# A planner's numbers for transfers are raised: longer issues, later landings of spreads and raw weights

## The chip, the cores and the metric

The kernel runs on one core of a Trainium2 chip. The metric is the time of one execution on the device, in microseconds (us). The core has five engines that work side by side, each through its own list of instructions, strictly in order: PE (matrix products), DVE (vector), ACT (activations), POOL (vector too, slower), and SP, which here only issues transfers (DMAs). An instruction whose input isn't ready holds up everything behind it on its engine.

## What is computed

```python
q_rot, k_rot = rotate(q), rotate(k)                    # 4 batches x 8 heads, 576 rows, 64 wide
attn = softmax(q_rot @ k_rot.T / sqrt(64)); a = attn @ v
x = a as [2304, 512]                                   # tokens x (heads * 64)
r = maximum(x @ w_in, 0.0);  g = s * (r * r) + b       # d_ff = 2048
x = g @ w_out
out = (silu(x @ w_gate) * (x @ w_val)) @ w_out2        # d_ff = 1536
```

## The kernel before

All products are made in pieces that keep nearly full precision: a number is split in a high part (hi) and a remainder (lo), and a product is two or three matmuls.

Attention works on 16 pairs of heads, pair 0 to pair 15. `prep` (a pair's preparation) loads q and k, rotates them (POOL from pair 1 on), transposes them on PE (pst, L515) and splits them: qkhi on ACT (L524), qklo on DVE (L526). Both lie in buffers of which there is one each. From there ten transfers on SP, the pair's *spread* (L548), copy the parts to where PE reads them: a, t and kz, two sets, used by even and odd pairs. The next pair's qkhi may be written only when the spread has landed; the token `hi` stands for that buffer. A spread also waits until the scores of two pairs before have been computed, since they read the same set.

`pair` then runs nine score blocks per pair: score matmuls into ps_s (L620), the row maximum nm on DVE (L623), the exponential e on ACT (L627). The probabilities are transposed on PE (ps_t, L681), split into ph on ACT (L689) and pl on DVE (L696), and multiplied with v (ps_av, L711), which ACT takes out as xr (L724) and SP stores to x_d (L732). The three PSUM banks of ps_t serve the transposes of q and k too.

The weights come as raw 64-bit numbers (`fetch`, L289 and L291, three raw buffers); ACT and DVE decode them (L304 to L315). Ten of the first MLP's are fetched during attention. The first MLP runs in five blocks of tokens; its input for the first block, xl and xh of 1 MB each, is loaded during attention (L762). The second MLP runs in three blocks.

The order is not written by hand. The kernel first describes every operation with its engine, a duration, what it needs, which buffers it takes and a priority (`op`, `dma`). `Schedule.run` then plays through them by these numbers: whenever an engine is free by the plan, it emits the ready operation of the best priority. The plan thus fixes the order of each engine's list, and nothing else; on the chip each instruction goes as soon as what it waits for is there. For a transfer the plan has SP busy for a fixed time, adds 0.65 us and the size over 360 KB per us (one transfer after the other), and 1.3 us until it has landed. A large pace makes a transfer count as larger.

Of the kernel before, what the change touches and what calls it, by code (L numbers as in the profile page):

```python
# [17 lines left out]


class Op:  # L20
    __slots__ = ("eng", "dur", "lag", "fn", "need", "users", "prio", "acq", "rel", "port", "ready", "done", "size", "next")


class Token:
# [6 lines left out]
class Schedule:  # L31
# [5 lines left out]
    def __init__(self):  # L37
        self.free, self.ops = {}, []

    def dma(self, size, fn, prio, deps=(), acq=(), rel=(), after=(), pace=1.0, eng="sp"):  # L40

        o = self.op(eng, 0.55, fn, prio, deps, acq, rel)
        o.size = size * pace
        for d in after:
            d.next.append(o)
            o.need += 1
        return o
# [15 lines left out]
    def run(self):  # L63
        ready = {}
        seq = 0
        wait = []
        for o in self.ops:
            if o.need == 0:
                heapq.heappush(wait, (0.0, seq, o))
                seq += 1  # L70
        busy = {}
        port_until = dma_free = 0.0
        work = {}
        times = [0.0]
        emitted = 0
        gone = []
        while times:
            now = heapq.heappop(times)
            while times and times[0] <= now + 1e-9:
                heapq.heappop(times)  # L80
            while gone and gone[0][0] <= now + 1e-9:
                _, _, o = heapq.heappop(gone)
                for t in o.rel:
                    t.left -= 1
                    if t.left == 0:
                        self.free[t.pool] += 1
            while wait and wait[0][0] <= now + 1e-9:
                _, s, o = heapq.heappop(wait)
                heapq.heappush(ready.setdefault(o.eng, []), (o.prio, s, o))
            for eng in sorted(ready, key=str):  # L90
                while busy.get(eng, 0.0) <= now + 1e-9 and ready[eng]:
                    skipped, got = [], None
                    while ready[eng]:
                        item = heapq.heappop(ready[eng])
                        o = item[2]
                        ok, picks = not (o.port and busy.get("pool", 0.0) > now + 1e-9 or eng == "pool" and port_until > now + 1e-9), []
                        for t in o.acq if ok else ():
                            p = next((p for p in t.pools if self.free.get(p, 0) - sum(x == p for _, x in picks) > 0), None)
                            if p is None:
                                ok = False  # L100
                                break
                            picks.append((t, p))
                        if ok:
                            got = o
                            break
                        skipped.append(item)
                        if len(skipped) > 60:
                            break
                    for item in skipped:
                        heapq.heappush(ready[eng], item)  # L110
                    if got is None:
                        break
                    o = got
                    for t, p in picks:
                        t.pool = p
                        self.free[p] -= 1
                    o.fn()
                    emitted += 1
                    dur = o.dur
                    if eng == "pe":  # L120
                        tick = int(now / 3.4133)
                        if work.get(tick - 1, 0.0) < 1.275:
                            dur *= 2
                        at = now
                        while at < now + dur:
                            tick = int(at / 3.4133 + 1e-9)
                            to = min(now + dur, (tick + 1) * 3.4133)
                            work[tick] = work.get(tick, 0.0) + (to - at) * o.dur / dur
                            at = to + 1e-9
                    end = now + dur  # L130
                    busy[eng] = end
                    if o.port:
                        port_until = end
                    o.done = end + o.lag
                    if o.size is not None:
                        dma_free = max(dma_free, end + 0.65) + o.size / 360e3
                        o.done = dma_free + 1.3
                    heapq.heappush(times, end)
                    seq += 1
                    heapq.heappush(times, o.done + RL)  # L140
                    heapq.heappush(gone, (o.done + RL, seq, o))
                    hop = self.HOP[eng] + self.HX if o.size is None else 0.0
                    for u, t in [(u, o.done + ((0.0 if u.eng == "pe" else 0.06) if u.eng == o.eng else hop)) for u in o.users] + [(u, end) for u in o.next]:
                        u.need -= 1
                        u.ready = max(u.ready, t)
                        if u.need == 0:
                            seq += 1
                            heapq.heappush(wait, (u.ready, seq, u))
                            heapq.heappush(times, u.ready)
        assert emitted == len(self.ops), (emitted, len(self.ops))  # L150
# [27 lines left out]
def tile_attention_moe_moe(  # L178
# [43 lines left out]
    sch = Schedule()  # L222
# [11 lines left out]
    late = {}  # L234
# [40 lines left out]
    def fetch(key, prio, dep=None, after=(), acq=()):  # L275

        kind, f = key
        src = {"in": w_in, "out": w_out, "gate": w_gate, "val": w_val, "out2": w_out2}[kind]
        wide = src.dtype != F32
        n = 2 if wide else 1  # L280
        if wide:
            src = src.bitcast(U32)
        st = {}
        raw_tok = Token("raw")

        def load():
            st["raw"] = raw = raw_p.tile([128, n * 512], U32 if wide else F32, tag="raw", name="raw")
            if kind in ("out", "out2"):
                nc.sync.dma_start(out=raw, in_=src[f * 128:(f + 1) * 128, :])  # L289
            else:  # L290
                nc.sync.dma_start(  # L291
                    out=raw.rearrange("p (k m) -> p k m", k=KD),
                    in_=src[:, f * 128 * n:(f + 1) * 128 * n].rearrange("(k p) m -> p k m", p=128),
                )

        o = W_ld[key] = sch.dma(n * 262144, load, prio, (dep,), (raw_tok, *acq), after=after, pace=1.5)
        if wide:
            dec_tok = Token("dec")

            def d0():  # L300
                two = st["raw"].rearrange("p (m two) -> p m two", two=2)
                st["low"], st["high"] = two[:, :, 0], two[:, :, 1]
                st["t"] = dec_p.tile([128, 512], U32, tag="dec", name="dec")
                nc.scalar.activation(out=st["t"].bitcast(F32), in_=st["high"].bitcast(F32), func=AF.Copy, scale=2.0 ** -112)  # L304

            def d1():
                nc.vector.tensor_scalar(out=st["t"], in0=st["t"], scalar1=3, scalar2=None, op0=ALU.logical_shift_left)

            def d2():
                nc.vector.scalar_tensor_tensor(  # L310
                    out=st["t"], in0=st["high"], scalar=0x80000000, in1=st["t"], op0=ALU.bitwise_and, op1=ALU.bitwise_or
                )

            def d3():
                nc.vector.scalar_tensor_tensor(  # L315
                    out=st["t"], in0=st["low"], scalar=29, in1=st["t"], op0=ALU.logical_shift_right, op1=ALU.bitwise_or
                )
                st["val"] = st["t"].bitcast(F32)

            o = op("act", t_act(512, False), d0, prio, (o,), (dec_tok,))  # L320
            o = op("dve", t_dve2(512), d1, prio, (o,), port=True)
            o = op("dve", t_dve(512), d2, prio, (o,), port=True)
            o = op("dve", t_dve(512), d3, prio, (o,), (), (raw_tok,), port=True)
            end = (dec_tok,)
        else:
            st["val"] = None
            end = (raw_tok,)
        return st, o, end
# [95 lines left out]
    def prep(p):  # L424
# [120 lines left out]
        if p > 1:  # L545
            def sp(o, i, first=False):
                return sch.dma(
                    256 * o.shape[1], lambda: nc.sync.dma_start(out=o.bitcast(F32), in_=i().bitcast(F32)), pr + 6, (*trs, *zeros[z]),  # L548
                    (tok,) if first else (), (hi_tok,), pace=1.3
                )  # L550
            ops = []
            for s0, s1, d0 in a_pieces(0, 2 * S):
# [819 lines left out]
```

## Time and profile before

| | us |
|---|---|
| median of 3 runs | 1133.8 (1132.83 to 1136.26) |
| the profiled execution | 1131.5 |
| its span | 1129.7 |
| PE busy | 1100.3 (97%) |
| DVE busy | 798.7 (71%) |
| ACT busy | 591.6 (52%) |
| POOL busy | 190.6 (17%) |

Attention takes about the first 300 us. POOL and the 16 DMA engines are busiest there: the DMA engines' busy share is 0.80 from 30 to 210 us. A wait is told as "engine, line, what it waited for". The clock of PE is given as a share of 2.4 GHz; its two levels are 1.2 and 2.4 GHz, 0.5 and 1.0 in the rows.

### The profile page before, as it was taken

The numbers are of one execution on the slowest core, as the hardware profiler recorded it, in microseconds if no ns is written. First come the engines' busy times: TensorE is split into PE (matmuls) and PEld (weight loads), VectorE is DVE, ScalarE is ACT, GpSimd is POOL, SyncE is SP. The second block draws the span as 40 slices with busy tenths as digits, with TensorE's granted clock in tenths as the row PEclk, the third lists the DMA queues.
The fourth block names the chain that finished last, engine by engine and source line by source line (L and its number), as shares of the span: only waits on it lengthen the run. The fifth ranks groups of instructions, "written<-read, shape, count | busy, mean of one in ns | idle before, by whom it ended". The sixth has DMA issues, their size and how long they took to land. (4 is left out here: it accounts for less than half of the span.)

```text
span 1129.7 us, 17997 instructions
## 1 busy us (share of the span) xinstructions
PE 1100.3 (97%) x6314; PEld 1006.1 (89%) x6314; DVE 798.7 (71%) x1394; ACT 591.6 (52%) x1199; POOL 190.6 (17%) x156
## 2 busy tenths in 40 slices
PE   7999899999999999999999999999999999999998
PEld 6989898989888788888899999999979999899986
DVE  6989888999969867867768764555565555665560
ACT  5989788889878845544554543322242222422230
POOL 6776675743200000000000000000000000000000
PEclk9999999999999999999999999999999999999999
DMA  5588888777376477576576766766656552666501
GB/s 125 135 197 182 219 210 200 187 168 186 88 236 190 127 231 233 177 238 222 196 241 217 250 225 209 247 201 206 210 158 221 197 195 96 196 229 194 183 11 46
DMA packets 185721, 211.16 MB, mean 187 GB/s; under 512 B 71824, under 2 KB 121120, under 8 KB 185632
## 3 DMA queue, kind: packets, MB, share of 16 engines
q1 hardware_dynamic: 184192, 209.33, 61.9%
q8 instruction: 50, 0.82, 0.3%
q10 hardware_dynamic: 1440, 0.69, 0.2%
q14 instruction: 39, 0.32, 0.1%
HBM read 142.07 MB, written 47.26 MB: 168 GB/s over the span
## 5 line engine op out<-in xcount | busy, mean ns | idle before, releaser
L1242 DVE TENSOR_TENSOR tmp<-hb,tmp 128x384 f32<-128x384 f32 x252 | 140.0, 557 | 114.0 <-PE hb L812 112.7
L810 PE MATMUL hb<-xh,w 128*128 128x384 f32 (+1 forms) x560 | 199.0, 355 | 2.0 <-DVE pl L696 2.0
L812 PE MATMUL hb<-xh,w 128*128 128x384 f32 (+1 forms) x560 | 199.0, 355 | 0.0
L811 PE MATMUL hb<-xl,w 128*128 128x384 f32 (+1 forms) x560 | 198.8, 355 | 0.0
L811 PE MATMUL acc<-gl,w 128*128 128x512 f32 (+1 forms) x320 | 117.9, 368 | 0.1
L810 PE MATMUL acc<-gh,w 128*128 128x512 f32 (+1 forms) x320 | 117.9, 368 | 0.0
L812 PE MATMUL acc<-gh,w 128*128 128x512 f32 (+1 forms) x320 | 117.6, 368 | 0.0
L810 PEld LDWEIGHTS hb<-xh,w 128*128 128x128 f32 x560 | 105.1, 188 | 12.7 <-DVE pl L696 1.5
L623 DVE TENSOR_REDUCE nm<-ps_s 128x1 f32<-128x576 f32 x144 | 108.2, 752 | 9.8 <-PE ps_s L620 8.7
L811 PEld LDWEIGHTS hb<-xl,w 128*128 128x128 f32 x560 | 105.1, 188 | 10.4
L627 ACT ACTIVATE e<-ps_s,nm 128x576 f32<-128x576 f32 x144 | 107.0, 743 | 10.8 <-DVE nm L623 10.0
L812 PEld LDWEIGHTS hb<-xh,w 128*128 128x128 f32 x560 | 105.1, 188 | 8.3 <-DVE w L349 0.2
L689 ACT ACTIVATE ph<-ps_t 128x512 fp32r<-128x512 f32 x192 | 106.7, 571 | 8.4 <-PE ps_t L681 6.3
L620 PE MATMUL ps_s<-t,a 128*128 128x288 f32 x320 | 101.2, 332 | 7.8 <-ACT e L627 7.8
L696 DVE TENSOR_TENSOR pl<-ps_t,ph 128x512 fp32r<-128x512 f32 x144 | 95.9, 683 | 5.9 <-ACT ph L689 5.3
L711 PE MATMUL ps_av<-ph,vh 128*128 128x384 f32 (+1 forms) x320 | 98.1, 328 | 0.0
L1257 ACT ACTIVATE tmp<-tmp 128x384 f32<-128x384 f32 x72 | 37.8, 525 | 111.5 <-DVE tmp L1242 109.2
L681 PE MATMUL ps_t<-ident,e 128*128 128x128 f32 x576 | 86.8, 276 | 6.9 <-DVE qklo L526 4.1
L620 PE MATMUL ps_s<-kz,a 128*128 128x288 f32 x320 | 90.7, 299 | 0.1
L811 PE MATMUL hb<-w 128*128 128x384 f32 x264 | 88.9, 337 | 0.0
L812 PE MATMUL hb<-w 128*128 128x384 f32 x264 | 88.8, 337 | 0.0
L810 PE MATMUL hb<-w 128*128 128x384 f32 x264 | 88.5, 335 | 0.0
(118 smaller groups left out, 2298.9 us busy)
## 6 DMA issues: line engine op xcount, KB each, us to landing
w<-wd SPq DMA_DIRECT2D x120, 512.0 KB, 4.4
wd<-w SPq DMA_DIRECT2D x48, 512.0 KB, 3.4
raw<-in_moe_w_out_dram SPq DMA_DIRECT2D x28, 512.0 KB, 5.1
x_d<-xr SPq DMA_DIRECT2D x64, 144.0 KB, 2.8
w<-wd SPq DMA_DIRECT2D x36, 256.0 KB, 4.0
raw<-in_moe_w_in_dram SPq DMA_DIRECT2D x16, 512.0 KB, 4.2
raw<-in_moe_w_gate_dram SPq DMA_DIRECT2D x12, 512.0 KB, 6.1
raw<-in_moe_w_val_dram SPq DMA_DIRECT2D x12, 512.0 KB, 6.3
```

The costliest lines, as they stand in the source:

```text
L620: nc.tensor.matmul(ps[:, hf * 512:hf * 512 + HS], a[:, q0:q0 + 128], m[:, k0:k0 + HS], start=y == 0, stop=y == len(todo) - 1)
L623: nc.vector.tensor_reduce(out=st["nm"][:, u:u + 1], in_=st["s", u], axis=AX.XY, op=ALU.max, negate=True)
L627: nc.scalar.activation(out=st["e", u].rearrange("p (f n) -> p f n", f=2), in_=st["s", u], func=AF.Exp, bias=st["nm"][:, u:u + 1], accum_ou ...
L681: nc.tensor.transpose(ps[:, z * 128:z * 128 + 128], st["e", u][:, kc * 128:kc * 128 + 128], ident)
L689: nc.scalar.activation(out=st["ph", y][0:rows, 512 * i:512 * i + n], in_=st["pt", y, i][0:rows, 0:n], func=AF.Copy)
L696: nc.vector.tensor_tensor(out=dst, in0=st["pt", y, i][0:rows, 0:n], in1=st["ph", y][0:rows, c].bitcast(F32), op=ALU.subtract)
L711: nc.tensor.matmul(ps, vv, st["ph", y][:, c], start=kc == 0, stop=kc == 4)
L810: nc.tensor.matmul(o, lh, rh, start=first, stop=False)
L811: nc.tensor.matmul(o, lh, rl, start=False, stop=False)
L812: nc.tensor.matmul(o, ll, rh, start=False, stop=last)
L1242: nc.vector.tensor_tensor(out=st[dst, f], in0=ps[z], in1=st[a, f], op=ALU.add)
L1257: nc.scalar.activation(out=st[key, f], in_=st[key, f], func=AF.Silu)
```

## The change

Three numbers of the plan change. Every transfer keeps SP busy for 0.64 us instead of 0.55. A transfer can have a `late`, which is added to its landing: 2.0 us for the ten transfers of each spread and for each raw weight, 0 for the rest. No operation is added or taken away, and no wait that data or buffers don't ask for.

```diff
-    __slots__ = ("eng", "dur", "lag", "fn", "need", "users", "prio", "acq", "rel", "port", "ready", "done", "size", "next")
+    __slots__ = ("eng", "dur", "lag", "fn", "need", "users", "prio", "acq", "rel", "port", "ready", "done", "late", "size", "next")
...
-    def dma(self, size, fn, prio, deps=(), acq=(), rel=(), after=(), pace=1.0, eng="sp"):
-
-        o = self.op(eng, 0.55, fn, prio, deps, acq, rel)
-        o.size = size * pace
+    def dma(self, size, fn, prio, deps=(), acq=(), rel=(), after=(), pace=1.0, eng="sp", late=0.0):
+
+        o = self.op(eng, 0.64, fn, prio, deps, acq, rel)
+        o.size, o.late = size * pace, late
...
                         dma_free = max(dma_free, end + 0.65) + o.size / 360e3
-                        o.done = dma_free + 1.3
+                        o.done = dma_free + 1.3 + o.late
...
-        o = W_ld[key] = sch.dma(n * 262144, load, prio, (dep,), (raw_tok, *acq), after=after, pace=1.5)
+        o = W_ld[key] = sch.dma(n * 262144, load, prio, (dep,), (raw_tok, *acq), after=after, pace=1.5, late=2.0)
...
-                    (tok,) if first else (), (hi_tok,), pace=1.3
+                    (tok,) if first else (), (hi_tok,), pace=1.3, late=2.0
```

The order of nearly the whole of attention changes, in the MLPs little. Three places follow. The numbers behind the names are buffers' numbers.

ACT, around the qkhi of pair 4. In the old order qkhi_1014 belongs to pair 4, and e_1131 is the first exponential of pair 3 (nm_1101 is pair 3's):

```order
L524 ACTIVATE qkhi_1014<-pst_1021,qs_203 128x2x192
L627 ACTIVATE e_1036,l_373<-ps_s_1008,nm_820 128x576
L724 ACTIVATE xr_864<-ps_av_967 128x384
L524 ACTIVATE qkhi_1014<-pst_1040,qs_203 128x2x192
L689 ACTIVATE ph_992<-ps_t_1048 128x512
L627 ACTIVATE e_1073,l_373<-ps_s_1027,nm_820 128x576
L689 ACTIVATE ph_992<-ps_t_1062 64x384
L689 ACTIVATE ph_1090<-ps_t_1080 128x512
L627 ACTIVATE e_1099,l_373<-ps_s_1055,nm_820 128x576
L689 ACTIVATE ph_1090<-ps_t_1093 128x512
L689 ACTIVATE ph_1090<-ps_t_1110 128x512
L627 ACTIVATE e_1131,l_373<-ps_s_1102,nm_1101 128x576
```

In the new order qkhi_1094 is pair 4's and nm_1076 is pair 3's:

```order
L689 ACTIVATE ph_1061<-ps_t_1034 128x512
L627 ACTIVATE e_1069,l_371<-ps_s_1046,nm_823 128x576
L689 ACTIVATE ph_1061<-ps_t_1063 128x512
L524 ACTIVATE qkhi_1094<-pst_1084,qs_203 128x2x192
L524 ACTIVATE qkhi_1094<-pst_1089,qs_203 128x2x192
L627 ACTIVATE e_1108,l_371<-ps_s_1077,nm_1076 128x576
L724 ACTIVATE xr_1117<-ps_av_1053 128x384
L524 ACTIVATE qkhi_1094<-pst_1110,qs_203 128x2x192
```

The three qkhi of pair 4 stood before the last exponentials of pair 2; now they stand around the first of pair 3.

PE, the transposes of q and k of pair 4 (pst) and the scores around them; a0 and t0 hold pair 2 here, a1 and t1 pair 3. Before:

```order
L681 MATMUL ps_t_994<-ident_201,e_855 128x128
L681 MATMUL ps_t_994<-ident_201,e_890 128x128
L515 MATMUL pst_1000<-ident_201,x_623 128x2x64 x3
L620 MATMUL ps_s_1008<-t0_206,a0_204 128x288
L620 MATMUL ps_s_1008<-kz0_208,a0_204 128x288
L620 MATMUL ps_s_1008<-t0_206,a0_204 128x288
L620 MATMUL ps_s_1008<-kz0_208,a0_204 128x288
```

Now, with the first score block of pair 3 at its head:

```order
L620 MATMUL ps_s_1077<-t1_207,a1_205 128x288
L620 MATMUL ps_s_1077<-kz1_209,a1_205 128x288
L620 MATMUL ps_s_1077<-t1_207,a1_205 128x288
L620 MATMUL ps_s_1077<-kz1_209,a1_205 128x288
L515 MATMUL pst_1084<-ident_201,x_615 128x2x64 x3
L515 MATMUL pst_1089<-ident_201,x_615 128x2x64 x3
```

The transposes of pair 4 moved from between the scores of pair 2 to behind the first scores of pair 3.

SP, around the spread of pair 6 (a0, t0, kz0) and the load of the first MLP block's input (xl, xh). Before, its last transfers and what follows:

```order
L548 DMA t0_206<-qklo_1496 64x576
L548 DMA kz0_208<-qkhi_1495 64x576
L732 DMA x_d00_126<-xr_1393 64x576
L732 DMA x_d10_130<-xr_1393 64x576
L762 DMA xl_1759<-x_d00_126 128x4x512
L762 DMA xh_1758<-x_d10_130 128x4x512
L732 DMA x_d01_127<-xr_1662 64x576
L732 DMA x_d11_131<-xr_1662 64x576
L392 DMA x_1792<-in_q_dram 128x9x64
L392 DMA x_1792<-in_k_dram 128x9x64
```

Now, what stands ahead of the same spread and its first transfers:

```order
L732 DMA x_d00_126<-xr_1381 64x576
L732 DMA x_d10_130<-xr_1381 64x576
L448 DMA vr_1545<-in_v_dram 64x2x64
L392 DMA x_1623<-in_q_dram 128x9x64
L392 DMA x_1623<-in_k_dram 128x9x64
L762 DMA xl_1647<-x_d00_126 128x4x512
L762 DMA xh_1646<-x_d10_130 128x4x512
L548 DMA a0_204<-qkhi_1587 64x576
L548 DMA a0_204<-qklo_1588 64x576
```

The two large loads moved from behind the spread of pair 6 to ahead of it.

## Rows read from the trace of the kernel before

**Rows 1.** Busy time by stage: start:end, length, each engine, clock, DMA share, GB/s.
```profile
30.00:210.00 180.00, 169.94 (x1291) 162.04 (x1290) 154.64 (x246) 154.03 (x364) 126.18 (x95) 0.98 0.80 191
210.00:300.00 90.00, 87.44 (x665) 82.15 (x664) 88.41 (x145) 82.29 (x196) 38.31 (x34) 1.00 0.68 164
316.00:808.00 492.00, 491.95 (x2442) 440.72 (x2442) 346.38 (x629) 239.33 (x415) 0.00 (x0) 1.00 0.66 216
```

**Rows 2.** Waits of PE, 30 to 210 us: total, times, longest, in us.
```profile
PE ps_t L681 <- DVE qklo L526: 4.1, 3, 2.9
PE ps_s L620 <- ACT e L627: 3.1, 4, 1.9
PE pst L515 <- DVE qklo L526: 2.6, 1, 2.6
```

**Rows 3.** Waits of ACT, 30 to 210 us.
```profile
ACT qkhi L524 <- DMA kz<-qkhi: 3.9, 2, 3.1
...
ACT qkhi L524 <- DMA t<-qklo: 3.3, 1, 3.3
ACT dec L304 <- DMA raw<-in_moe_w_in_dram: 2.1, 1, 2.1
```

**Rows 4.** Timeline of PE: start, length, instruction, idle before it and its releaser.
```profile
129.54 0.60 PE L681 MATMUL ps_t<-ident,e 128*128 128x128 f32 x4
129.90 0.38 PE L620 MATMUL ps_s<-t,a 128*128 128x288 f32 x1
...
137.40 1.12 PE L681 MATMUL ps_t<-ident,e 128*128 128x128 f32 x4 [2.92 <-DVE qklo L526]
...
157.29 0.40 PE L620 MATMUL ps_s<-t,a 128*128 128x288 f32 x1 [1.86 <-ACT e L627]
```

**Rows 5.** Busy time and clock after the two stalls, columns as in rows 1.
```profile
136.00:144.00 8.00, 6.61 (x40) 6.33 (x40) 6.01 (x10) 7.21 (x17) 2.68 (x5) 0.79 0.84 197
156.00:164.00 8.00, 6.71 (x38) 6.44 (x39) 6.04 (x10) 6.48 (x17) 4.41 (x5) 0.79 0.66 140
```

**Rows 6.** Timeline of SP's queue around the spread of pair 6.
```profile
92.24 0.59 SPq L548 DMA_DIRECT2D kz<-qkhi  x1
...
99.87 0.78 SPq L392 DMA_DIRECT2D x<-in_k_dram  x1
...
103.08 0.60 SPq L548 DMA_DIRECT2D a<-qkhi  x1
...
108.86 0.60 SPq L548 DMA_DIRECT2D kz<-qkhi  x1
...
113.44 1.99 SPq L732 DMA_DIRECT2D x_d<-xr  x2
...
116.18 1.97 SPq L392 DMA_DIRECT2D x<-in_k_dram  x1
118.21 3.44 SPq L446 DMA_DIRECT2D vr<-in_v_dram  x1
...
123.02 0.62 SPq L444 DMA_DIRECT2D vr<-in_v_dram  x1
...
125.68 1.18 SPq L732 DMA_DIRECT2D x_d<-xr  x2
```

**Rows 7.** Line 548, the spreads: time from issue to landing.
```profile
DMA to landing us min/median/max: 2.4/3.0/5.3
```

**Rows 8.** ACT's instructions of attention: count, duration, and qkhi's first and last start.
```profile
L627 ACT ACTIVATE e<-ps_s,nm 128x576 f32<-128x576 f32 x144 | 107.0, 743 | 10.8 <-DVE nm L623 10.0
L689 ACT ACTIVATE ph<-ps_t 128x512 fp32r<-128x512 f32 x192 | 106.7, 571 | 8.4 <-PE ps_t L681 6.3
...
L724 ACT ACTIVATE xr<-ps_av 128x384 f32<-128x384 f32 x48 | 23.8, 497 | 0.5 <-PE ps_av L711 0.5
...
L524 ACT ACTIVATE qkhi<-pst,qs x42: 567/582/607, 36.3 to 262.6; 128x384 fp32r<-128x384 f32 x42
```

## The prediction

> **What bounds the kernel now.** I read the busy time by stage first, then PE's waits, then the waits of the engine that PE waited for, then SP's queue.
>
> The stages [rows 1]: from 316 to 808 us PE is busy for 491.95 of 492.00 us at the full clock. There no other order can save anything. Attention is different. From 30 to 210 us PE is busy for 169.94 of 180.00 us, so 10.06 us are idle, and the granted clock is 0.98. From 210 to 300 us it idles for 2.56 of 90.00 us. DVE is busy 154.64 of the 180 us, and 88.41 of the 90: behind PE it is the next limit.
>
> Who holds PE up between 30 and 210 us [rows 2]: 4.1 + 2.6 = 6.7 us end with qklo on DVE, and 3.1 us with the exponentials on ACT. These are chains. PE's transposes wait for a bank of PSUM that qklo has to empty, qklo waits for qkhi on ACT, and qkhi waits for a DMA: the previous pair's spread has not landed, and qkhi must overwrite the buffer that the spread reads. ACT's own list says so [rows 3]: 3.9 us for kz<-qkhi, 3.3 us for t<-qklo, and 2.1 us in which the decode waited for a raw weight. The largest of these stalls on PE are 2.92 us before 137.40 and 1.86 us before 157.29 [rows 4]. PE is slow after both: in the 8 us from 136 and the 8 us from 156 the mean granted clock is 0.79, partly the lower of its two levels [rows 5].
>
> SP is what makes the spreads late. From the first to the last of one spread's ten issues there are nine steps in 108.86 - 103.08 = 5.78 us, 0.64 us each [rows 6], where the plan of before reckons 0.55: 0.9 us too little for ten. A spread transfer lands a median of 3.0 us from its issue, 5.3 us at worst [rows 7].
>
> **The change part by part.** It adds no instruction; the planner only writes the same ones down in another order.
>
> *Spreads.* The planner now reckons 10 x 0.09 = 0.9 us more issue and 2.0 us more landing, so everything that needs a spread moves back by about 2.9 us. On ACT, between the last qkhi of pair 3 and the first of pair 4, the old order holds 1 qkhi, 8 ph, 6 e and 2 xr: 0.58 + 8 x 0.57 + 6 x 0.74 + 2 x 0.50 = 10.6 us [rows 8]. The new one holds 1, 11, 8 and 2: 13.8 us. That is 3.2 us more cover, and the wait there was the 3.1 us one [rows 3]. Pairs 3 to 5 had 10.6 to 11.7 us in this tally and have 13.8 now. On PE the new order puts the q and k transposes of pair p behind the first scores of pair p - 1, which need the spread of p - 1 complete. So qkhi can hardly wait for a landing any more. I count the whole 6.7 us as gone, and with the stall the slow clock after it: 8 x 0.21 = 1.7 us [rows 5]. Bounds: 0 (the wait moves to the scores) to 8.4 us; I take 8.4, since the added cover equals the measured wait.
>
> *Raw weights.* In the old order the first decode is ACT's next instruction behind the qkhi of pair 9. In the new one it stands nine instructions behind the qkhi of pair 8: 3 e, 5 ph, 1 xr, 5.6 us [rows 8], against a wait of 2.1 us [rows 3]. The PE stall of 1.86 us goes, and its clock, 1.7 us: 3.6 us, between 0 and 3.6. In the MLPs the same 2.0 us changes nothing that PE waits for [rows 1].
>
> *What comes late next.* First, the first MLP block's x: two transfers, xl and xh. They were issued behind the spread of pair 6; now they stand ahead of it, in front of ten transfers with no slack. In the old run the transfers behind them went out slowly [rows 6]: the x_d pair took 1.99 us (1.18 at 125.68), the k load 1.97 (0.78 at 99.87), the v load 3.44 (0.62 at 123.02): 0.8 + 1.2 + 2.8 = 4.8 us too much. From the end of the spread of pair 5 to the start of the next SP needed 103.08 - 92.83 = 10.25 us, now three issues more (1.6 us); then ten issues (6.4), the 4.8, and 2.4 to land (3.0 less one issue): 25.4 us. PE can start the scores of pair 5 when its spread has landed (2.4) and by the new plan does so some 2.0 later. A pair takes PE 16.6 us: busy 257.4 of 270 us [rows 1], at 17.4 us a pair (ACT's qkhi of 14 pairs start over 226 us [rows 8]). Between the scores of pairs 5 and 6 the new order has some twenty more transposes of probabilities at 0.09 us (four from 129.54 to 129.90 [rows 4]), 1.8 us. Scores of pair 6 are thus reached at 2.4 + 2.0 + 16.6 + 1.8 = 22.8 us: a stall of 2.6 us. Bounds: 0 if SP is not slowed, 4.6 + 1.7 us of clock if PE has no lag. I take 2.6.
>
> Second, the other engines. From 210 to 300 us, with hardly any such wait, PE still idles 2.8% [rows 1]. On 180 us that is 5.1 us, where 10.06 - 6.7 - 1.86 = 1.5 us would be left: 3.6 us come back. Bounds 0 and 3.6; I take 3.6, because DVE at 155 of some 170 us comes close to its load of the later stretch.
>
> Sum: 8.4 + 3.6 - 2.6 - 3.6 = 5.8 us off the profiled execution's 1131.5 us: 1125.7. That execution lies 2.3 us under the median of the runs, 1133.8, so the median forecast is 1128.0 us.
>
> On the landings the Trainium skill has a rule that speaks against a fixed allowance: in "DMA: Bandwidth & Descriptors", Latency and other measured facts, it gives 0.2 us for an access to HBM on average and 2 us at high load, so that the fixed cost of a transfer grows with load. The trace agrees that landings spread widely, 2.4 to 5.3 us around 3.0 [rows 7]. By that rule 2.0 us is too much for most spreads and too little behind a burst. It would make the next rival likelier.
>
> **The rivals.**
> *The wait only moves (1129 to 1137).* The late landing follows the bursts. With the scores next behind each landing, PE stalls itself where ACT did. For it: SP issues almost without a pause from 92 to 134 us [rows 6], and the new order leaves the scores no slack. Against it: the three early waits had no burst near. If half of the gain of 12.0 us is lost on top of the 6.2 above, nothing is left: 1133.8.
>
> *Slower.* SP decides. A pair needs 24 or 25 issues; at 0.64 us that is 15.4 to 16.0, and with the slow ones of [rows 6] up to 20, against PE's 16.6. In the old order a pair's scores stood well behind the next pair's transposes, and that distance absorbed it. In the new one each excess is PE's at once. It decides from the point where SP takes over 17.4 us a pair; with 2 us for each of pairs 6 to 11, and one more clock loss of 1.7 for two of them, 12 + 3.4 stand against a gain of 12.0 - 3.6: 7 us slower, 1141.
>
> *All goes (1121.8).* No new wait appears: 12.0 us off. For it: PE's busy time allows it. Against it: DVE's load.
>
> *The change does nothing in the MLPs*, as all my terms suppose; were it to open a new wait there, rows 1 show none to start from.
>
> **How the numbers follow.** The three runs of before lie within 1132.83 to 1136.26, so less than 0.3% (3.4 us) can't be told from no change. Forecast of 1128.0: 0.45; all goes: 0.17; the wait only moves: 0.22; slower: 0.16. Faster takes the forecast but for its upper edge (0.42), all of the third and a little of the wait that moves (0.03): 0.62. The same: the edge (0.03) and most of the wait that moves (0.18): 0.21. Slower: the 0.16 and 0.01 of the wait that moves, 0.17. The range runs from 1120 (all goes, with the early waits of the first 30 us a little shorter) to 1139 (most of the slower case); the forecast's own is 1123 to 1131.
>
> **What would show it.** Right: qkhi's waits for DMA on ACT fall from 7.2 us to under 2; PE's waits for qklo from 6.7 to under 1.5; the clock is 1.00 in all slices from 130 to 165 us; PE waits for an a, t or kz spread once, at pair 6; attention gives way to the MLP 5 to 7 us earlier, and PE's busy time in the MLPs stays. Wrong: PE idles for DMA before the scores of several pairs, or stalls with ACT's exponentials grow as those for qklo fall, or the MLP stages show new idle time.

## The result and the profile after

The changed kernel takes 1141.4 us (median of 4 runs, 1140.28 to 1142.46) against 1133.8: a ratio of 1.0060, with a 95% interval of 1.0043 to 1.0076. It is slower by about 7 us where 6 us faster was forecast, and it lies outside the forecast's range of 1120 to 1139. Its profiled execution took 1142.46 us, with a span of 1140.7.

First the stages, as in [rows 1], with the seam of attention and MLP and three windows of the first MLP block added. Windows of the changed kernel, columns as in [rows 1]:

```profile
30.00:210.00 180.00, 168.82 (x1277) 161.20 (x1276) 156.39 (x245) 154.59 (x362) 120.31 (x92) 0.98 0.79 188
210.00:300.00 90.00, 87.74 (x663) 82.15 (x662) 87.91 (x141) 82.14 (x193) 43.77 (x38) 1.00 0.66 165
300.00:316.00 16.00, 13.72 (x87) 12.21 (x86) 14.67 (x28) 12.38 (x29) 3.85 (x3) 0.89 0.32 96
316.00:808.00 492.00, 487.24 (x2401) 433.24 (x2401) 344.20 (x620) 240.72 (x418) 2.59 (x2) 1.00 0.65 211
360.00:380.00 20.00, 19.03 (x82) 14.82 (x80) 17.93 (x33) 15.06 (x26) 0.00 (x0) 1.00 0.56 175
380.00:400.00 20.00, 16.51 (x67) 12.12 (x67) 15.85 (x28) 13.77 (x25) 0.00 (x0) 1.00 0.44 142
400.00:420.00 20.00, 19.70 (x84) 15.07 (x83) 8.02 (x13) 10.76 (x18) 0.00 (x0) 1.00 0.65 206
```

The same three last windows of the kernel before:

```profile
360.00:380.00 20.00, 20.00 (x89) 16.22 (x88) 18.95 (x36) 17.67 (x31) 0.00 (x0) 1.00 0.60 192
380.00:400.00 20.00, 19.95 (x87) 15.88 (x86) 12.45 (x21) 13.55 (x23) 0.00 (x0) 1.00 0.43 129
400.00:420.00 20.00, 20.00 (x88) 16.10 (x87) 13.72 (x26) 11.06 (x19) 0.00 (x0) 1.00 0.62 207
```

The MLPs, which were full in [rows 1], have lost 4.8 us of PE's time, all of it here: 82 + 67 + 84 = 233 matmuls in these 60 us where there were 89 + 87 + 88 = 264. At 60 / 264 = 0.227 us each, the 31 missing are 7.0 us. Of these 4.8 us are idle time; the rest lies in the 233 matmuls, which take 0.237 us on the mean. Before, PE waited for nothing that the profile lists from 316 to 730 us; now its list of waits there is (total, times, longest):

```profile
PE acc L810 <- ACT gh L867: 1.8, 1, 1.8
PE hb L810 <- ACT w L342: 1.4, 3, 0.7
PE acc L811 <- DVE gl L872: 1.0, 2, 0.8
PE hb L812 <- DVE w L349: 0.6, 1, 0.6
```

w is a decoded weight split in its two parts; gh and gl are made of what PE computes with it. So weights come late, and it isn't their landing that is late. ACT's waits for the last step of a decode, from 316 to 420 us, in the kernel before

```profile
ACT w L342 <- DVE dec L315: 2.8, 4, 2.0
```

and in the changed kernel, where in the same stretch no decode waits for a transfer:

```profile
ACT w L342 <- DVE dec L315: 15.8, 13, 2.1
```

SP's timeline of the kernel before, the last two weights of the first MLP:

```profile
379.15 0.37 SPq L291 DMA_DIRECT2D raw<-in_moe_w_in_dram  x1
382.95 0.34 SPq L289 DMA_DIRECT2D raw<-in_moe_w_out_dram  x1
```

and the same two transfers of the changed kernel, 11 to 12 us later:

```profile
391.05 0.37 SPq L291 DMA_DIRECT2D raw<-in_moe_w_in_dram  x1
394.23 0.34 SPq L289 DMA_DIRECT2D raw<-in_moe_w_out_dram  x1
```

In attention the forecast waits went and others came. PE's waits from 30 to 210 us in the changed kernel, answering to [rows 2]:

```profile
PE ps_s L620 <- ACT e L627: 3.9, 2, 2.4
PE ps_av L711 <- ACT xr L724: 2.9, 1, 2.9
PE ps_t L681 <- DVE qklo L526: 2.3, 3, 1.2
```

ACT's waits there, answering to [rows 3]:

```profile
ACT xh L797 <- POOL xs L793: 7.7, 3, 3.3
...
ACT qkhi L524 <- DMA x_d<-xr: 1.4, 1, 1.4
```

The profile names no spread in qkhi's waits any more (7.2 us before). The names are inferred: in the built lists of both kernels (each engine's instructions with the waits that they carry) the only transfers that qkhi waits for are a spread's, so the 1.4 us put down to x_d are a spread's too, and all of qkhi's waits for transfers went from 9.9 to 1.4 us. The decode no longer waits for a weight (2.1). In their place ACT stands 7.7 us at xh, the first MLP block's input; before, that was 0.4. xh needs xs from POOL, and POOL waits for the rows of reciprocals that normalise it, in the changed kernel

```profile
POOL xs L793 <- DMA rbx<-r_d: 16.5, 6, 4.3
```

against, before,

```profile
POOL xs L793 <- DMA rbx<-r_d: 6.3, 6, 2.2
```

How that reaches PE is seen on two timelines of the changed kernel (in brackets: idle before it and its releaser). ACT:

```profile
130.42 0.63 ACT L797 ACTIVATE xh<-xs 128x512 fp32r<-128x512 f32 x1 [3.26 <-POOL xs L793]
130.96 0.47 ACT L724 ACTIVATE xr<-ps_av 128x384 f32<-128x384 f32 x1
...
165.67 0.63 ACT L797 ACTIVATE xh<-xs 128x512 fp32r<-128x512 f32 x1 [2.08 <-POOL xs L793]
...
202.34 0.63 ACT L797 ACTIVATE xh<-xs 128x512 fp32r<-128x512 f32 x1 [2.38 <-POOL xs L793]
```

and PE, to be read beside [rows 4]:

```profile
131.49 0.45 PE L711 MATMUL ps_av<-ph,vh 128*128 128x384 f32 x1 [2.90 <-ACT xr L724]
...
167.56 0.40 PE L620 MATMUL ps_s<-t,a 128*128 128x288 f32 x1 [1.46 <-ACT e L627]
...
204.12 0.40 PE L620 MATMUL ps_s<-t,a 128*128 128x288 f32 x1 [2.41 <-ACT e L627]
```

xr stands behind xh in ACT's list, and PE needs the bank that xr empties: 2.90 us, as long as the largest stall of [rows 4]. At 167.56 and 204.12 it is an e that stands behind xh. The three together are 6.8 of the 11.2 us that PE idles from 30 to 210 us. The slow clock moves with them. Windows of the changed kernel, behind the first and the third stall and at the two places of [rows 5]:

```profile
132.00:136.00 4.00, 4.00 (x22) 3.89 (x21) 3.56 (x6) 2.55 (x6) 1.90 (x2) 0.61 1.04 243
136.00:144.00 8.00, 7.94 (x58) 7.36 (x58) 6.54 (x12) 7.33 (x18) 8.00 (x6) 0.98 0.74 184
156.00:164.00 8.00, 6.75 (x54) 6.49 (x54) 7.17 (x12) 5.89 (x14) 6.46 (x4) 1.00 0.62 156
204.00:208.00 4.00, 3.88 (x19) 3.87 (x20) 2.64 (x4) 3.06 (x8) 1.76 (x2) 0.57 0.99 222
```

From 136 and from 156 us the clock is back at its upper level (0.98 and 1.00); 4 x 0.39 = 1.6 us are lost from 132 us and 4 x 0.43 = 1.7 us from 204 us instead.

**Where attention ends.** The last product with v tells it. The row of line 711 in the kernel before:

```profile
L711 PE MATMUL ps_av<-ph,vh x320: 247/335/669, 23.2 to 314.0; 128*128 128x384 f32 x80, 128*128 128x192 f32 x80
```

and in the changed one:

```profile
L711 PE MATMUL ps_av<-ph,vh x320: 249/336/668, 30.3 to 316.9; 128*128 128x384 f32 x80, 128*128 128x192 f32 x80
```

PE has done 15 matmuls of the MLP by then before, 6 after, so the second figure is to be read as 316.9 + 9 x 0.227 = 318.9. Three more profiles below (e6, e11, e5) have the order of before in attention: they end it at 318.0, 319.6 and 320.6. The profiled execution of before was the best of four; their mean is 318.1. So attention shows no gain (0.8 us later, well inside the scatter of the four), and the loss is that of the MLP block: 0.8 + 7.0 = 7.8 us.

### The profile page after: what moved, and what is told of

Read it like the earlier page. It is cut to its first block, busy times and chain, and to the rows that moved or that the text cites. A ratio compares the mean times of both kernels' runs of the same rounds, so it can differ in the third digit from the quotient of the medians.

```text
span 1140.7 us, 17988 instructions
## 1 busy us (share of the span) xinstructions
PE 1107.3 (97%) x6314; PEld 1010.3 (89%) x6314; DVE 804.3 (71%) x1394; ACT 593.3 (52%) x1199; POOL 190.0 (17%) x156
## 4 chain that ended last, share of the span: by engine, by line
PE 81%; DVE 8%; ACT 5%; DMA 2%; issue 2%; POOL 1%; SPq 1%; POOLq 0%; ACTq 0%; DVEq 0%
PE hb L812 13%; PE hb L811 13%; PE hb L810 13%; PE acc L811 5%; PE acc L812 5%; PE acc L810 5%; PE acc L1174 4%; PE acc L1176 4%; PE acc L1175 4%; PE ps_s L620 4%; PE ps_t L681 3%; PE ps_av L711 2%; DVE nm L623 2%; DVE pl L696 2%; PE ps_av L713 2%
## 5 line engine op out<-in xcount | busy, mean ns | idle before, releaser
L623 DVE TENSOR_REDUCE nm<-ps_s 128x1 f32<-128x576 f32 x144 | 108.0, 752 | 15.8 <-PE ps_s L620 14.7
L810 PEld LDWEIGHTS hb<-xh,w 128*128 128x128 f32 x560 | 105.1, 188 | 12.7 <-ACT w L342 2.7
L711 PE MATMUL ps_av<-ph,vh 128*128 128x384 f32 (+1 forms) x320 | 102.7, 341 | 5.7 <-ACT xr L724 3.2
L620 PE MATMUL ps_s<-t,a 128*128 128x288 f32 x320 | 98.7, 325 | 7.4 <-ACT e L627 6.8
```

Of the source, the lines that this page charges most:

```text
L620: nc.tensor.matmul(ps[:, hf * 512:hf * 512 + HS], a[:, q0:q0 + 128], m[:, k0:k0 + HS], start=y == 0, stop=y == len(todo) - 1)
L623: nc.vector.tensor_reduce(out=st["nm"][:, u:u + 1], in_=st["s", u], axis=AX.XY, op=ALU.max, negate=True)
L711: nc.tensor.matmul(ps, vv, st["ph", y][:, c], start=kc == 0, stop=kc == 4)
L810: nc.tensor.matmul(o, lh, rh, start=first, stop=False)
```

## Experiments

Each kernel was timed beside the kernel before on the same chip (medians there 1135.9 to 1136.4), so the ratios are to be compared. The table has all; the end of attention is corrected as above, to 15 matmuls.

| kernel | issue | spreads | weights, attention / MLP | rbx | attention ends | matmuls 360 to 420 | ratio (95%) |
|---|---|---|---|---|---|---|---|
| before | 0.55 | 0 | 0 / 0 | 0 | 314.0 | 264 | 1 |
| after | 0.64 | 2.0 | 2.0 / 2.0 | 0 | 318.9 | 233 | 1.0060 (1.0043 to 1.0076) |
| e1 | 0.64 | 0 | 0 / 0 | 0 | 322.3 | 269 | 1.0026 (1.0012 to 1.0041) |
| e2 | 0.55 | 2.0 | 0 / 0 | 0 | 317.9 | 265 | 0.9987 (0.9970 to 1.0004) |
| e3 | 0.55 | 0 | 2.0 / 2.0 | 0 | 322.7 | 236 | 1.0094 (1.0070 to 1.0119) |
| e4 | 0.64 | 2.0 | 0 / 0 | 0 | 316.2 | 268 | 0.9998 (0.9982 to 1.0013) |
| e5 | 0.55 | 0 | 0 / 2.0 | 0 | 320.6 | 220 | 1.0079 (1.0062 to 1.0096) |
| e6 | 0.55 | 0 | 0 / 1.0 | 0 | 318.0 | 253 | 1.0025 (1.0013 to 1.0038) |
| e11 | 0.55 | 0 | 0 / -0.5 | 0 | 319.6 | 263 | 0.9999 (0.9989 to 1.0010) |
| e7 | 0.64 | 2.0 | 2.0 / 0 | 0 | 319.1 | 261 | 1.0029 (1.0015 to 1.0043) |
| e8 | 0.64 | 2.0 | 2.0 / 0 | 2.0 | 316.6 | 262 | 1.0053 (1.0037 to 1.0069) |
| e12 | 0.64 | 2.0 | 2.0 / 0 | 2.0, first block | 316.6 | 269 | 0.9981 (0.9968 to 0.9994) |
| e9 | 0.55 | 2.0 | 2.0 / 0 | 0 | 321.9 | 269 | 1.0019 (1.0008 to 1.0030) |
| e10 | 0.55 | 1.0 | 0 / 0 | 0 | 315.7 | 265 | 0.9978 (0.9967 to 0.9989) |

**The parts alone.** e1, issues of 0.64 us only (from the changed kernel):

```diff
-        o = W_ld[key] = sch.dma(n * 262144, load, prio, (dep,), (raw_tok, *acq), after=after, pace=1.5, late=2.0)
+        o = W_ld[key] = sch.dma(n * 262144, load, prio, (dep,), (raw_tok, *acq), after=after, pace=1.5)
...
-                    (tok,) if first else (), (hi_tok,), pace=1.3, late=2.0
+                    (tok,) if first else (), (hi_tok,), pace=1.3
```

> Of the change only the issue time of 0.64 us is kept; no transfer has a later landing. Theory A (the loss of 7 us between 360 and 420 us comes from the later landing of raw weights, the rest from attention's order): the first MLP block runs without PE waits for weights, its last weight is issued within 3 us of the 382.95 us of before, and the time is 1131 to 1137. Rival B (the longer issue thins out the plan's supply of weights): PE waits for weights between 360 and 400 us as in the changed kernel, 4 us or more, and the time is 1138 to 1142.

e2, the spreads only:

```diff
-        o = self.op(eng, 0.64, fn, prio, deps, acq, rel)
+        o = self.op(eng, 0.55, fn, prio, deps, acq, rel)
...
-        o = W_ld[key] = sch.dma(n * 262144, load, prio, (dep,), (raw_tok, *acq), after=after, pace=1.5, late=2.0)
+        o = W_ld[key] = sch.dma(n * 262144, load, prio, (dep,), (raw_tok, *acq), after=after, pace=1.5)
```

> Only the later landing of the spreads is kept; issue 0.55, raw weights as before. Theory A: qkhi's waits for a spread go (7.2 us before, under 2 here), no PE wait for weights in the first MLP block; 1127 to 1134. Rival B: 1127 to 1134 too, so this run tells only how the spreads' part stands: if it is over 1137, the order with late spreads costs attention time by itself (rival C).

e3, the raw weights only: 0.55 as in e2, and the spreads' late=2.0 taken away.

> Only the later landing of raw weights is kept. Theory A: PE waits for weights in the first MLP block as in the changed kernel, 4 to 8 us lost between 360 and 420 us, 1137 to 1143. Rival B (issue) and rival C (attention's order): no such loss, 1131 to 1136.

e4, the changed kernel without late=2.0 for the raw weights.

> The changed kernel without the later landing of raw weights: issue 0.64 and spreads late by 2.0 us. Theory A: the 7 us of the first MLP block come back, 1132 to 1137, and attention ends like the changed kernel's or a little earlier. Rival B: the loss stays, 1139 to 1143.

Measured: the raw weights alone cost 0.94%, more than the whole change, and without them nothing is lost (0.9998). In e3, 28 matmuls are missing from 360 to 420 us, and attention ends late too. The longer issue alone costs 0.26%: in attention qkhi still waits 9.7 us for spreads, and from 420 to 808 us, where PE idles for nothing before or in the changed kernel, it idles 2.4 us, mostly for ACT's r (L856). The other kernels below with issues of 0.64 us (e4, e7, e12) lose 1.4 to 2.2 us there too; those with 0.55 lose none. The spreads alone bring 0.13%, hardly told from nothing. In e2 qkhi's waits for a spread fall to 0.2 us, as forecast, but the decode behind a raw weight now waits 4.7 us on ACT and PE 6.0 us for exponentials.

**The weights in the MLP.** e5 is the kernel before with the allowance for the 22 weights of the first MLP that are fetched after attention, and nothing else; up to the end of attention its order is that of before:

```diff
-        o = W_ld[key] = sch.dma(n * 262144, load, prio, (dep,), (raw_tok, *acq), after=after, pace=1.5)
+        o = W_ld[key] = sch.dma(n * 262144, load, prio, (dep,), (raw_tok, *acq), after=after, pace=1.5, late=2.0 if kind in ("in", "out") and not after else 0.0)
```

> The kernel before with a single edit: the 22 weights of the first MLP that are fetched after attention get the later landing of 2.0 us. Up to about 300 us the order of every engine is that of before, word for word. Theory A (in the plan a raw buffer is then held 2 us longer, each decode moves back in the lists of ACT and DVE, and PE reaches the weights before they are decoded): 5 to 9 us slower than before, all of it lost between 360 and 420 us, last weight issued about 393 us. Rival D (the loss in the changed kernel needs attention's late end, not the weights' numbers): within 2 us of before.

e6 is the same with 1.0 in place of 2.0, and e11 with -0.5.

> The same with 1.0 us instead of 2.0. Theory A: the loss needs the decodes to move back further than the weights are ahead of PE; with half the number it is well under half, 0 to 4 us. Rival D: within 2 us of before.

> The kernel before with late -0.5 (landing reckoned 0.5 us earlier) for the 22 weights of the first MLP that are fetched after attention; the order up to the end of attention is that of before. With 2.0 the same edit cost 9 us, with 1.0 2.9 us. Theory A (it is the late reckoning that thins the supply of weights): no loss, ratio 0.998 to 1.001, and 87 to 91 matmuls in each of the windows 360:380, 380:400 and 400:420. Theory B (any other order in the first block costs, because the old one happened to be good): 2 to 4 us slower, ratio 1.0015 to 1.0035, and one of the three windows has under 80 matmuls.

Windows of e5, to be read beside those of before:

```profile
360.00:380.00 20.00, 18.48 (x75) 14.40 (x74) 18.32 (x34) 14.77 (x26) 0.00 (x0) 0.94 0.53 163
380.00:400.00 20.00, 16.70 (x65) 11.86 (x64) 15.23 (x27) 13.64 (x24) 0.00 (x0) 0.97 0.47 145
400.00:420.00 20.00, 19.09 (x80) 14.97 (x81) 8.15 (x14) 9.86 (x17) 0.00 (x0) 1.00 0.51 164
```

44 matmuls are missing (10.0 us), and the time is 0.79% or 9.0 us longer. With 1.0 us it is 2.9 us, with -0.5 nothing (0.9999), though the order on DVE and ACT differs there as well: it isn't any other order that costs, but a landing reckoned too late. The built lists show what that does. Told by the gl operations ahead of them in DVE's list, the decodes of 15 of the 22 weights stand one place later than before in e5, 6 in e6, and in e11 3 later and 1 earlier. e6 is the neatest case: PE's list is word for word that of before, and only the places of the decodes on DVE and ACT, with the work beside them, and of nine transfers on SP differ. The last of the 22 weights goes out 69.0 us after the last product with v before, 68.2 in e11, 71.3 in e6, 77.2 in e5 (77.3 in the changed kernel).

**The new wait in attention.** e7 is the changed kernel with the allowance for the ten weights fetched in attention alone:

```diff
-        o = W_ld[key] = sch.dma(n * 262144, load, prio, (dep,), (raw_tok, *acq), after=after, pace=1.5, late=2.0)
+        o = W_ld[key] = sch.dma(n * 262144, load, prio, (dep,), (raw_tok, *acq), after=after, pace=1.5, late=2.0 if after and kind in ("in", "out") else 0.0)
```

> The changed kernel, with the later landing of raw weights kept only for the ten that are fetched during attention. Theory A: the first MLP block runs without PE waits for weights, as in the run without later raw weights; the wait of the decode for a raw weight during attention (3.4 us there) goes, so the time is that run's or up to 4 us less: ratio to before 0.995 to 1.000. Rival C (attention's order with late spreads loses by itself, in the waits of xh for xs, 7 us): over 1.002.

e8 adds the allowance for the loads that POOL's xs waits for:

```diff
-                last = sch.dma(512 * (c1 - c0), ld, prio + kk, deps, (rb_tok,) if z == 0 else (), after=(last,))
+                last = sch.dma(512 * (c1 - c0), ld, prio + kk, deps, (rb_tok,) if z == 0 else (), after=(last,), late=2.0)
```

> The same, and the loads of rbx (the row sums by which the first MLP block's x is scaled) get the later landing of 2.0 us too. In the changed kernel they landed late: POOL waited for them, ACT's xh waited for POOL for 7.7 us, and PE for ACT. Theory E (this wait took the place of the spreads'): ACT's wait for xs falls under 2 us, the clock stays 1.00 after 128 us, and the time falls 2 to 6 us under that of the run before it. Rival: PE's idle time in attention stays within 1.5 us, since another wait comes up.

e12 gives it to the first block alone, whose loads run in attention:

```diff
-                last = sch.dma(512 * (c1 - c0), ld, prio + kk, deps, (rb_tok,) if z == 0 else (), after=(last,), late=2.0)
+                last = sch.dma(512 * (c1 - c0), ld, prio + kk, deps, (rb_tok,) if z == 0 else (), after=(last,), late=2.0 if x_eng == "pool" else 0.0)
```

> The run with raw late only in attention and late 2.0 for all rbx loads, with one thing changed: the rbx allowance now holds for the first block of the first MLP alone (its loads run during attention), 0 for the other blocks. The order of attention stays what it was there. Theory A (in attention the wait of xh for rbx was what took the freed time; the loss of that run came in the later blocks alone, 6.9 us before 653 us and the slow clock after it, mean 0.78 over 20 us, 4.4 us): attention ends within 2 us of 313.2, the PE wait for xh in the later blocks is gone, and the time falls by 11 us to 1131, a ratio of 0.994 to 0.998. Theory B (whatever is freed in attention is lost again in the first MLP block): attention ends as early, but 12 or more matmuls are missing in the windows 360:380, 380:400 and 400:420 (264 before), and the ratio is 1.000 to 1.005. Theory C (the early end of attention in that one profile was luck): attention ends after 316, ratio 0.999 to 1.004.

e7 gets the 28 matmuls back, and half of the loss: 1.0029. It keeps the order of the changed kernel in attention and its wait (8.6 us of xh for xs). In e8 that wait is 2.2 us, attention ends 2.5 us sooner than in e7, and yet the kernel is slower. PE's timeline of e8 shows why:

```profile
653.49 0.69 PE L810 MATMUL hb<-xh,w 128*128 128x384 f32 x1 [6.92 <-ACT xh L797]
```

The same allowance put the input of a later block too late, and its window from 650 us shows the slow clock behind the stall:

```profile
650.00:670.00 20.00, 16.45 (x78) 15.83 (x79) 14.72 (x28) 9.91 (x19) 0.00 (x0) 0.78 0.79 274
```

e12 has the attention of e8, without that stall. Its row of attention, the fullest of all profiles:

```profile
30.00:210.00 180.00, 170.62 (x1296) 160.75 (x1296) 161.86 (x251) 155.62 (x365) 117.98 (x89) 1.00 0.79 187
```

It is 0.19% faster than before (0.06 to 0.32%): the wait for rbx was what the change lacked in attention, the weights what it had too much of in the MLP. The loads themselves land no sooner for it: POOL still waits 17.5 us for rbx (15.6 in e7), but ACT's xh now stands behind other work and waits 2.5. The forecast of 1131 was too good (1134.5).

**Less of it.** e9 is e7 with the issue at 0.55; e10 is e2 with 1.0 for the spreads in place of 2.0.

> Issue back at 0.55; late 2.0 for the spreads and for the ten raw weights that are fetched in attention; 0 for the first MLP's other weights. The run with the spreads' allowance alone was 0.13% faster than before and had one new stall in attention, the decode behind a raw weight (4.7 us on ACT, 6.1 us on PE behind the exponentials). Theory A (the early raw allowance removes that stall, and what it frees reaches PE): the decode's wait on ACT falls under 1 us, PE's wait for e from 6.1 to under 4, and the time is 3 us under that run: ratio to before 0.994 to 0.998. Theory B (freed stalls are replaced): the decode's wait goes, but another wait of 3 us or more stands on ACT (xh behind POOL's xs, or qkhi behind a DMA), and the ratio is 0.998 to 1.003.

> Issue 0.55, raw weights 0, late 1.0 instead of 2.0 for the spreads. Theory A (the gain comes from spreads that are there in time, and 1.0 us covers most landings): qkhi's waits for a spread on ACT stay under 1.5 us (7.2 before), and the ratio to before is 0.996 to 0.999. Theory B (the order is a lottery: each new order brings other waits): qkhi's waits fall as well, but the ratio lies anywhere from 0.998 to 1.004 without relation to them; a ratio above 1.001 speaks for it.

e9 was to be better than e2 and is worse: the decode waits 1.2 us instead of 4.7, but attention ends 4 us later, with stalls of up to 2.5 us scattered over PE's list. The second theory foretold it: ACT's xh now waits 5.8 us for xs, 1.4 in e2. e10 is 0.22% faster than before (0.11 to 0.33%), although qkhi still waits 4.0 us for spreads by the profile's names (8.0 for transfers in all). So the time doesn't follow this wait. e10 and e12 are the two kernels that beat the one before clear of their intervals; the runs don't tell them apart, and of a dozen tried two by so little can owe something to chance.

## Why the prediction was wrong

*The step that failed* is the end of the paragraph on raw weights: "In the MLPs the same 2.0 us changes nothing that PE waits for". It was worth about 7 of the 13.4 us between forecast and result; the rest is attention, where 5.8 us of gain were forecast and none came. It rested on [rows 1], where PE is full from 316 to 808 us. That shows that the old order kept up, not how much slack the supply of weights had. With three raw buffers, a weight that the plan takes to land 2.0 us late is decoded late in the plan; its decode then stands behind other work in the lists of ACT and DVE, and there the chip does it late too, though the data are there: 15.8 us of ACT's waits for a decode against 2.8, and none of a decode for its transfer. The buffer comes free late, and the next transfer with it. A size that the trace could have given was missing as well: the plan of before already reckons 0.55 + 0.65 + 2.2 + 1.3 = 4.7 us from a weight's issue to its landing (2 x 262144 bytes x 1.5 / 360 KB per us = 2.2). The loads and decodes of the raw weights in the trace of before, 316 to 420 us, end with

```profile
DMA to landing us min/median/max: 3.5/4.0/8.7
```

Nothing was late in the median; with 2.0 more the plan was wrong by 2.7 us. The last rival came nearest: "were it to open a new wait there, rows 1 show none to start from". It had neither a price nor a chance.

*Spreads, 8.4 us.* The wait went nearly as forecast: qkhi's for a spread from 7.2 us to under 2, PE's for qklo from 6.7 to 2.3, where under 1.5 was set, and the clock at the places of [rows 5] is back. What the sum made of it was wrong: 6.7 us of stall taken away did not make PE 6.7 us earlier. It idles 11.2 us from 30 to 210 us, 10.1 before, 6.8 of them behind xh, and the slow clock came back at other places. Alone, the spreads gave 1.5 us (e2) to 2.5 (e10). "The wait only moves" was right on attention, but not at the scores, as that rival had it: it moved to xh, an instruction that the list of ACT's waits before had at 0.4 us, and that the sum had no term for.

*Raw weights in attention, 3.6 us.* The decode's wait went, and yet the allowance costs 0.31% there (e4 to e7) and 0.32% (e2 to e9). In both pairs attention ends later, by 2.9 and 4.0 us, and xh's wait for xs is longer, 8.6 us for 7.0 and 5.8 for 1.4. How much of the cost that is isn't shown: the other stalls are small and change from place to place.

*The burst, 2.6 us lost at pair 6.* The spread went out as late as feared, but not for the reason given, and PE lost nothing by it. SP's timeline of the changed kernel, answering to [rows 6]:

```profile
105.38 0.82 SPq L762 DMA_DIRECT2D xl<-x_d  x1
106.30 0.44 SPq L762 DMA_DIRECT2D xh<-x_d  x1
106.83 0.97 SPq L548 DMA_DIRECT2D a<-qkhi  x1
...
112.62 0.46 SPq L548 DMA_DIRECT2D kz<-qkhi  x1
116.83 0.46 SPq L548 DMA_DIRECT2D t<-qkhi  x1
117.46 0.47 SPq L548 DMA_DIRECT2D t<-qklo  x1
118.19 0.46 SPq L548 DMA_DIRECT2D kz<-qkhi  x1
```

The spread takes 11.8 us to issue, where 6.4 + 4.8 = 11.2 were reckoned. That the numbers agree is luck: the 4.8 stood for slow single issues, and here each takes 0.97 us or less. What holds the list up are two waits:

```profile
SPq L548 <- DMA xh<-x_d: 3.7, 1, 3.7
...
SPq L548 <- DMA xl<-x_d: 1.4, 1, 1.4
```

The kz at 112.62 is the eighth transfer behind xl, the t at 116.83 the eighth behind xh. In the built lists of both kernels the transfers use eight semaphores in turn, and nearly every one waits until the one eight places ahead has landed. So there is a wait that neither data nor buffers ask for; the plan doesn't reckon it, and a new order of SP's list changes which transfers it couples. But PE has no stall for it: it is busy 8.00 of 8.00 us from 104 to 112 and from 112 to 120, at the full clock, with other work of the list. Line 548 as a whole, beside [rows 7]:

```profile
DMA to landing us min/median/max: 2.6/3.8/10.6
```

The median landing went from 3.0 to 3.8 us and the longest from 5.3 to 10.6 with the same transfers in another order. No fixed allowance fits both ends, and 1.0 did no worse than 2.0. The Trainium skill's rule in "DMA: Bandwidth & Descriptors", Latency and other measured facts, by which the fixed cost of a transfer grows with the load on HBM, points the same way. No run here tests it: a spread goes from one buffer on the chip to another, and the mean busy share of the DMA engines from 30 to 210 us is 0.80 before and 0.79 now.

*Other engines, 3.6 us,* can't be told from the new waits. In e12, where each of those waits is small, PE still idles 9.4 us from 30 to 210 us, more than the 5.1 that this term left; and from 210 to 300 us it idles 4.6 us where it was 2.6, so a fuller first part was followed by an emptier one.

*The slower rival* has the right time, 1141, by the wrong way: SP was to decide, and of PE's waits from 30 to 210 us none is for a spread.

*The base.* The sum was made against one execution. Four of the same order, on more than one chip, end attention between 314.0 and 320.6 us, with PE's waits for qklo between 6.7 and 9.6 us, and the one shown was the best of them. A gain of 5.8 us in attention can't be read from one such profile against another; that takes the medians of many runs.

## What to carry to other kernels

A number in a planner is an allowance for a measured lateness: work out what the plan already reckons for that transfer and set it beside the trace's time from issue to landing, stage by stage, before more is added. A stage in which the bound engine never waits shows that its order works, not that it has slack, and an allowance there moves whatever refills a short ring of buffers. And where one wait is taken from a list, look at the next instruction on that engine whose input comes by a transfer: its allowance has to move as well, there only.

## What was not expected of the hardware

A single issue on SP can itself take long behind large transfers. In [rows 6], behind xl and xh, the load of k took 1.97 us and one of v 3.44, where others like them took 0.78 and 0.62. Why isn't shown; the 4.2 us between 112.62 and 116.83 in the changed kernel are no such thing but the wait for xh told above.

Identical lists of instructions up to 300 us leave PE 6.6 us apart at their end in four executions (318.0 and 320.6 are of one chip). With it goes how long qkhi waits for transfers, which by the built lists are a spread's: 9.9 us from 30 to 210 us in the one that ends at 314.0, 12.7 to 13.2 in the other three. What makes the same spreads land later isn't shown. The runs' times as a whole lie within 0.7% on one chip.
